# A planned attention and gated feed-forward kernel: new rules for the order of down's sums and of the weight pieces, two more v tiles, and an output weight that is split in the middle of the run

## The chip, the cores and the metric

The kernel runs on one core of one Trainium2 chip. The metric is the time of one execution in microseconds on the device, as the median of several runs. The core's engines are TensorE (PE in the profile, with its weight loads as PEld), VectorE (DVE), ScalarE (ACT), GpSimd (POOL) and SyncE (SP, which here issues nearly all transfers, in one order).

## What is computed

The input x has 2048 rows of 576 numbers, in fp32.

```python
xn = layernorm(x)
q, k, v = split(xn @ wqkv)                    # 32 heads of 18 columns
s = concat(softmax(q @ k.T * 18**-0.5) @ v) @ wo
g = silu(((xn @ w_gate) * (xn @ w_up)) @ w_down)   # inner width 4608
out = x + s * g
```

## The kernel before, in words

Every fp32 operand of a product is held as a high and a low part (`hi` is a rounded copy, made by ScalarE; `lo` is the rest, made by a subtraction on GpSimd or VectorE), and a product is the sum of hi·hi, lo·hi and hi·lo.

**Prologue.** x is normalised and turned into columns, q, k and v are computed with the whole array (`qk_block`, `v_block`). The 16 blocks of v come in the order 0 to 3, 8 to 15, 4 to 7; block t goes through one of three SBUF tiles, `vbox[t % 3]` (L389), is copied there by ScalarE (L391) and stored to `sv` by SP (L393). Between those stores SP also issues the loads of x's columns in their two-half layout (`x_first`, L417).

**Main phase.** `order()` (L1046) is a planner that runs while the program is built. It keeps a modelled clock for each of the two row halves of TensorE's array (`clk[0]`, `clk[1]`), a modelled time at which each other engine is free (`free`) and at which each PSUM bank is free (`banks`), and writes out the matmuls one after another. The work that it places:

- *gate and up*, in 72 units (4 chunks of 512 rows by 18 groups of 256 inner columns) of two column blocks n each. Up runs on half 0 (`up_end`, ScalarE drains the bank), gate on half 1 (`gate_end`, VectorE multiplies, then ScalarE and GpSimd split the product into `hs`). One block is 27 matmuls of 512 columns per half (L618).
- *down*, 8 sums per unit, each of 6 matmuls of 288 columns on half 0 and then 6 on half 1 into the same bank (L664). An instruction on a third engine (L668) hands the bank from one half to the other. `down_end` drains the bank: VectorE adds to `acc` (L721), or ScalarE copies (L715) and GpSimd adds (L684).
- *a items*: scores for the row maxima, mostly on half 0 (L530; VectorE reduces, L532). *b items*: the scores again, mostly on half 1 (L569; ScalarE takes the exponential, L571). Each kind has two PSUM banks of its own. a and b are paced by goals (`a_goal`, `b_goal`) so that they last over the whole phase.
- *visits*: up to six blocks of probabilities times v, on the whole array (L580).

Gate, up, down and visits share four PSUM banks (`banks["g"]`). `pick` (L1032) chooses between the streams of one half: it prefers gate or up while `54 * (g's unit - d's unit - 1) + 27 * (block) + step < FROM + STEP * sum`, with `FROM, STEP = 54, 0`; otherwise down. `can_go` (L982) says what may start; a new sum of down waits while three of the four banks are held or more than one sum is being handed over (`WAITING`).

**Weights.** In the first 18 units the weights come raw from HBM. A list, `chores`, holds their splitting in pieces: three per gate/up block (L205, L206), two per down unit (L236, L237), each followed by a step that stores the split tile for the later chunks and loads the next raw one (L211, L241). `small` (L912) takes one from the list when the modelled ScalarE is free within 0.1 us:

```python
eng, length = KINDS.get(q[0][0].__name__, ("POOL", 0.0))
if eng == "POOL" or free[eng] <= now + 0.1 + (0.15 * (now - quiet[0]) if q is later else 0.0):
```

When a matmul is written that needs weights whose pieces have not been placed, `ready` (L159) places them all at that point, without telling the modelled clocks (`gu_start`, L611; `down_start`, L657). A second list, `later`, holds less urgent steps (`silu`).

**End.** After the last gate block, `wo_prepare` (L761) loads the output weight raw and splits it on ScalarE (L771) and VectorE (L772). Then 16 blocks of rows are projected (L1187), multiplied and added (L1197, L1198), and stored.

Of the kernel before, what the change touches and what calls it, by code (L numbers as in the profile page):

```python
# [40 lines left out]
def kernel(  # L41
# [34 lines left out]
    sv = dram.tile([S, H, DH + 1], FT, name="sv")  # L76
    so = dram.tile([S, D], FT, name="so")
    sg = dram.tile([S, D], FT, name="sg")

    turns = [0]  # L80

# [63 lines left out]


    chores, later = [], []

    def chore(all=True):
        q = (all and chores) or later  # L150
# [30 lines left out]
    def g_get(n):  # L181

        if n == 2 * len(units):
            u = n // 2 - 1
            dw[u] = wpool.tile([128, 2, 2, D], FR, name="wdl", tag="wgu", bufs=2)
            nc.sync.dma_start(dw[u].bitcast(FT), swd[columns_of(u)])
            ddone.add(u)
        if n >= 2 * len(units):
            return
        f = 2 * columns_of(n // 2) + n % 2  # L190
        if n > 1 and n // 2 % NF2 == 0:
            gw[n] = gw[n - 2]
            gdone.add(n)
            return
        w = gw[n] = g_tile()
        if n >= 2 * NF2:
            nc.sync.dma_start(w.bitcast(FT), swg[f])
            gdone.add(n)
            return
        if n not in graw:  # L200
            ready(gdone, n - 2)
        raw = graw.pop(n)

        def piece(b):
            nc.scalar.activation(w[:, b:b + 3, :], raw[:, b:b + 3, :], AF.Copy)  # L205
            nc.gpsimd.tensor_tensor(w[:, 9 + b:12 + b, :], raw[:, b:b + 3, :], w[:, b:b + 3, :].bitcast(FT),  # L206
                                    op=OP.subtract)

        def end():
            gdone.add(n)  # L210
            nc.sync.dma_start(swg[f], w.bitcast(FT))  # L211
            g_load(n + 2)

        chores.extend([(piece, (b,)) for b in (0, 3, 6)] + [(end, ())])
# [5 lines left out]
    def d_get(n):  # L220
        if n >= len(units) - 1:
            return
        p = columns_of(n)
        if n and n % NF2 == 0:
            dw[n] = dw[n - 1]
            ddone.add(n)
            return
        w = dw[n] = d_tile()
        if n >= NF2:
            nc.sync.dma_start(w.bitcast(FT), swd[p])  # L230
            ddone.add(n)
            return
        raw = draw.pop(n)

        def piece(k):
            nc.scalar.activation(w[:, k, 0, :], raw[:, k], AF.Copy)  # L236
            nc.gpsimd.tensor_tensor(w[:, k, 1, :], raw[:, k], w[:, k, 0, :].bitcast(FT), op=OP.subtract)  # L237

        def end():
            ddone.add(n)  # L240
            nc.sync.dma_start(swd[p], w.bitcast(FT))  # L241
            d_load(n + 1)

        chores.extend([(piece, (k,)) for k in range(2)] + [(end, ())])

    R = 3 * DH
    PT = 13
# [109 lines left out]
    vbox = {}  # L357

    def v_fetch(h):
        raw = vp.tile([128, 5, HALF], FT, name="wvraw", bufs=1)  # L360
# [7 lines left out]
    def v_split(h):  # L368
        if h == 0:
            vbox["w"] = vp.tile([128, 10, D], FR, name="wv")  # L370
            for i in range(3):
                vbox[i] = vp.tile([128, H, DH + 1], FT, name=f"vo{i}")
                nc.gpsimd.memset(vbox[i], 1.0)
        raw, wv = vbox["raw"], vbox["w"]
        cs = slice(h * HALF, (h + 1) * HALF)
        for k, d, lo in ((0, 0, 4), (1, 1, 5), (2, 2, 6), (3, 3, 7), (4, 8, 9)):
            nc.scalar.activation(wv[:, d, cs], raw[:, k, :], AF.Copy)
            nc.gpsimd.tensor_tensor(wv[:, lo, cs], raw[:, k, :], wv[:, d, cs].bitcast(FT),
                                    op=OP.subtract)

    def v_block(t):
        c, r = divmod(t, 4)
        ps = [bank("g", 3), bank("g", 3)]
        for h in range(2):
            for n, (a, e) in enumerate(PAIRS):
                nc.tensor.matmul(ps[h][:, 0:HALF], xcs[c][:, e, r * 128:(r + 1) * 128],  # L386
                                 vbox["w"][:, a, h * HALF:(h + 1) * HALF], start=n == 0,
                                 stop=n == len(PAIRS) - 1)
        v = vbox[t % 3]  # L389
        for h in range(2):  # L390
            nc.scalar.activation(v[:, 16 * h:16 * h + 16, 0:DH],  # L391
                                 ps[h][:, 0:HALF].rearrange("p (a b) -> p a b", b=DH), AF.Copy)
        nc.sync.dma_start(sv[t * 128:(t + 1) * 128], v)  # L393
# [68 lines left out]
    for i in range(2):  # L462
        qs.append(stk.tile([128, S], FR, name=f"qs{i}"))
        ks.append(stk.tile([128, S], FR, name=f"ks{i}"))
        nc.gpsimd.memset(ks[i].bitcast(FT), 1.0)
    g_load(0)
    g_load(1)
    d_load(0)
# [29 lines left out]
    for t in range(4, 8):  # L498
        v_block(t)
        chore()  # L500
    assert n == 18
    pro.close()
    vstack.close()

# [7 lines left out]
    with ExitStack() as mid:  # L512
# [106 lines left out]
                             stop=k == len(TERMS) - 1)  # L619

        def up_end(n, ps):
            us[n] = mp.tile([128, 512], FT, name="us", bufs=1)
            nc.scalar.activation(us[n], ps, AF.Copy)  # L623

# [99 lines left out]
        def down_summed(u, s):  # L724
            c, q = units[u]
            if q == NF2 - 1 and c < NCH - 1:
                seen[c, s] = seen.get((c, s), 0) + 1
                if seen[c, s] == 2:
                    silu_store(4 * c + s)

        def silu(t, new, end):

# [25 lines left out]

        wos = {}

        def wo_prepare():  # L761
            raw = xcp.tile([128, 8, D], FT, name="wor", tag="xc")
            nc.sync.dma_start(raw[:, 0:4, :], wo[0:512, :].rearrange("(k p) c -> p k c", p=128))
            for b in (0, 64):
                nc.sync.dma_start(raw[b:b + 64, 4, :], wo[512:576, :])
            wos[0] = xcp.tile([128, 8, D], FR, name="wos", tag="xc")
            wos[1] = wpool.tile([128, 2, D], FR, name="wos2", tag="wgu", bufs=2)

            def piece(k):
                hi, lo = (wos[0][:, k, :], wos[0][:, 4 + k, :]) if k < 4 else (wos[1][:, 0, :], wos[1][:, 1, :])  # L770
                nc.scalar.activation(hi, raw[:, k, :], AF.Copy)  # L771
                nc.vector.tensor_tensor(lo, raw[:, k, :], hi.bitcast(FT), op=OP.subtract)  # L772

            chores.extend([(piece, (k,)) for k in range(5)])

        passed = {}

        def stream(r, kind):

            def glu(n):  # L780
                c, q = units[n // 2]
                box = []
                for k in range(len(TERMS)):
                    def work(k=k):
# [6 lines left out]
                        if k == len(TERMS) - 1:  # L791
                            (gate_end if r else up_end)(n, box[0])
                            if r and n == 2 * len(units) - 1:
                                wo_prepare()
# [31 lines left out]
        TOTAL = H * N  # L826
        LEAD, MOST, AHEAD, MANY = 24, 40, PT - 1, 6
        PACE, SKEW, PULL, FIRST = 1.005, 1.0, 3.0, 0.4
        FROM, STEP, WAITING = 54, 0, 1
        slots, gone = {}, [0.0, 0.0]  # L830
        clk, free = [0.0, 0.0], {"DVE": 0.0, "ACT": 0.0, "POOL": 0.0}
        banks = {"a": [0.0] * 2, "b": [0.0] * 2, "g": [0.0] * 4}
        turn = {"a": 0, "b": 0}

# [30 lines left out]
        def a_next(r=0):  # L865
# [7 lines left out]
            a_item(h, i, r)  # L873
            slot = turn["a"] % 2
            turn["a"] += 1
            banks["a"][slot] = engine("DVE", clk[r] + 0.45, 0.70) + 0.06
            clk[r] += 0.229
            na += 1
            if i == N - 1:
# [8 lines left out]
        def b_next(r=1):  # L888
# [10 lines left out]
            slot = turn["b"] % 2  # L899
            turn["b"] += 1  # L900
            end = engine("ACT", clk[r] + 0.45, 0.60)
            banks["b"][slot] = end + 0.06
            clk[r] += 0.229
            nb += 1
            if i % 4 == 3:
                due.append((h, i // 4, end + 0.1))

        KINDS = {"piece": ("ACT", 0.55), "first": ("ACT", 0.70), "second": ("DVE", 0.45), "inverse": ("DVE", 1.06)}

        quiet = [0.0]  # L910

        def small(now):  # L912

            q = chores or later
            if q is later and now < quiet[0]:
                return
            if q:
                eng, length = KINDS.get(q[0][0].__name__, ("POOL", 0.0))
                if eng == "POOL" or free[eng] <= now + 0.1 + (0.15 * (now - quiet[0]) if q is later else 0.0):
                    if eng != "POOL":  # L920
                        done = engine(eng, now, length)
                        if q[0][0].__name__ == "piece":
                            engine("POOL", done + 0.1, 1.05)
                    elif q[0][0].__name__ == "last":
                        engine("POOL", now, 1.5)
                    if not chores:
                        quiet[0] = now + (16.0 if q[0][0].__name__ == "last" else 6.0)
                    chore()

        def rows(job):  # L930
# [48 lines left out]

        upped, gated, downed = {}, {}, {}  # L980

        def can_go(r, first, ev):  # L982

            kind, n, k = ev
            now = clk[r]
            if kind == "d":
                if r and not alone(n, k // 6):
                    return k % 6 or handed.get((n, k // 6), 1e9) <= now
                if first and (sum(t >= 1e9 for t in banks["g"]) >= 3 or len(handed) > WAITING):
                    return False  # L990
                return k or (there.get(("h", n), 1e9) <= now and (n < 1 or downed.get(n - 1, 1e9) <= now))
            u = n // 2
            c, q = units[u]
            if k == 0:
                if n > 1 and loaded.get(n - 2, 1e9) > now:
                    return False
                if r and ahead[0] - ahead[1] < FIRST and heads[0]["g"] is not None:
                    return False
# [231 lines left out]
```

## Time and profile before

| | us |
|---|---|
| median of 3 runs | 2736.94 (2736.72 to 2739.9) |
| the profiled execution | 2743.11 |
| its span, first to last instruction | 2741.1 |
| busy: PE, PEld | 2666.4, 2181.3 |
| busy: DVE, ACT, POOL | 1825.9, 1571.0, 651.9 |

How to read it: a busy PE is not a PE at its peak. With two halves of the array at work, an instruction of one half alone counts as busy as one of each. The row PEclk tells the clock that TensorE was granted in each slice of the span. In the views quoted below, "A <- B: t, n, m" says that A waited for B t microseconds in total, n times, m at the longest; a row of the view by stage has, for each engine, busy microseconds with the number of instructions in brackets, then granted clock, share of the DMA engines, and GB/s.

### The profile page before, as it was taken

What the parts mean: (1) busy time and instruction counts of PE and PEld (TensorE: products, weight loads), DVE (VectorE), ACT (ScalarE), POOL (GpSimd) and SP (SyncE); (2) the same over time, 40 slices, a digit from 0 to 9 for tenths busy, and PEclk for the clock granted to TensorE, in tenths of its full rate; (3) what the DMA queues carried; (4) which work ended last, traced back from release to release, by engine and by line L of the source; (5) the groups of instructions that cost most, each with busy time, mean ns of one, the idle gap of its engine ahead of it and who ended that gap; (6) DMA issues with size and microseconds to landing.
All of it is one profiled execution on the core that took longest, in us unless ns stands there. A gap on an engine that the chain in (4) does not pass through costs nothing.

```text
span 2741.1 us, 59194 instructions
## 1 busy us (share of the span) xinstructions
PE 2666.4 (97%) x24504; PEld 2181.3 (80%) x24504; DVE 1825.9 (67%) x3012; ACT 1571.0 (57%) x3096; POOL 651.9 (24%) x671
## 2 busy tenths in 40 slices
PE   7998999989899999999999999999999999999999
PEld 6897887767677887788778778888887888887779
DVE  7207776656566777776677777777777777777336
ACT  4222666656565666566655666666666666666652
POOL 3113534433331111111111112111111122211115
PEclk9999999989899999999999999999999999999999
DMA  7797757756565453544454445444456444443346
GB/s 218 228 288 213 209 152 198 191 147 147 163 155 152 133 149 124 144 131 124 146 137 133 124 151 147 140 140 137 146 138 151 138 144 136 144 144 108 122 141 215
DMA packets 199805, 428.40 MB, mean 156 GB/s; under 512 B 80976, under 2 KB 130544, under 8 KB 166128
## 3 DMA queue, kind: packets, MB, share of 16 engines
q1 hardware_dynamic: 197296, 416.36, 51.4%
q0 software_dynamic: 2240, 8.26, 0.8%
q8 instruction: 192, 3.15, 0.5%
q14 instruction: 77, 0.63, 0.1%
HBM read 311.69 MB, written 107.61 MB: 153 GB/s over the span
## 4 chain that ended last, share of the span: by engine, by line
PE 92%; DMA 3%; DVE 2%; SPq 1%; ACT 1%; POOL 1%; issue 1%; POOLq 0%; ACTq 0%; DVEq 0%
PE pg L618 33%; PE pg L580 17%; PE pg L664 15%; PE pa L530 11%; PE pb L569 9%; PE pg L1187 2%; PE pg L386 2%; PE pa L332 1%; PE pb L332 1%; SPq L417 1%; DMA wgu<-swg 1%; POOL wd L237 1%; DMA ks<-sqk 1%; ACT pt L571 0%; DVE xn L294 0%
## 5 line engine op out<-in xcount | busy, mean ns | idle before, releaser
L532 DVE TENSOR_REDUCE mx<-pa 128x1 f32<-128x512 f32 x2048 | 1374.9, 687 | 350.9 <-PE pa L530 199.9
L618 PE MATMUL pg<-xc,wgu 64*128 64x512 f32 x7776 | 1478.3, 396 | 24.7 <-ACT vo L391 12.3
L571 ACT ACTIVATE pt<-pb 128x512 f32<-128x512 f32 x2048 | 1168.0, 597 | 560.3 <-PE pb L569 399.9
L618 PEld LDWEIGHTS pg<-xc,wgu 64*128 64x128 f32 x7776 | 1093.9, 188 | 70.5 <-ACT vo L391 12.6
L664 PE MATMUL pg<-wd,hs 64*128 64x288 f32 x6816 | 886.5, 297 | 19.9 <-ACT wd L236 10.1
L664 PEld LDWEIGHTS pg<-wd,hs 64*128 64x128 f32 x6816 | 814.9, 188 | 42.5 <-POOL wd L237 14.3
L569 PE MATMUL pb<-qs,ks 56*128 56x512 f32 x2048 | 814.5, 407 | 0.3 <-ACT pt L571 0.2
L530 PE MATMUL pa<-ks,qs 54*128 54x512 f32 x2048 | 809.4, 403 | 0.0
L580 PE MATMUL pg<-pt,vt 128*32 128x512 f32 x4096 | 463.9, 599 | 6.0 <-DVE us L630 2.7
L530 PEld LDWEIGHTS pa<-ks,qs 54*128 54x128 f32 x2048 | 374.8, 186 | 77.7 <-issue 66.2
L640 POOL TENSOR_TENSOR hs<-us,hs 128x512 fp32r<-128x512 f32 x144 | 185.8, 1290 | 991.2 <-ACT hs L633 806.7
L569 PEld LDWEIGHTS pb<-qs,ks 56*128 56x128 f32 x2048 | 372.5, 185 | 25.9 <-ACT pt L571 10.8
L684 POOL TENSOR_TENSOR acc<-acc,st 128x288 f32<-128x288 f32 x268 | 216.2, 808 | 617.2 <-ACT st L715 324.5
L580 PEld LDWEIGHTS pg<-pt,vt 128*32 128x32 f32 x4096 | 123.9, 110 | 288.7 <-issue 272.9
L586 DVE TENSOR_TENSOR oc<-oc,pg 128x512 f32<-128x512 f32 x64 | 44.0, 687 | 306.7 <-PE pg L580 306.7
L633 ACT ACTIVATE hs<-us 128x512 fp32r<-128x512 f32 x144 | 91.0, 632 | 118.9 <-DVE us L630 118.7
L721 DVE TENSOR_TENSOR acc<-acc,pg 128x288 f32<-128x288 f32 x277 | 123.5, 447 | 48.1 <-PE pg L664 43.9
L206 POOL TENSOR_TENSOR wgu<-wraw,wgu 128x384 fp32r<-128x384 f32 x108 | 107.5, 1012 | 195.0 <-ACT wgu L205 145.2
L630 DVE TENSOR_TENSOR us<-pg,us 128x512 f32<-128x512 f32 x144 | 98.7, 685 | 50.0 <-PE pg L618 40.4
L715 ACT ACTIVATE st<-pg 128x288 f32<-128x288 f32 x268 | 109.9, 410 | 37.3 <-PE pg L664 22.8
L623 ACT ACTIVATE us<-pg 128x512 f32<-128x512 f32 x144 | 85.8, 595 | 39.5 <-PE pg L618 34.0
L584 ACT ACTIVATE oc<-pg 128x512 f32<-128x512 f32 x32 | 19.1, 598 | 132.8 <-PE pg L580 132.8
(105 smaller groups left out, 1148.9 us busy)
## 6 DMA issues: line engine op xcount, KB each, us to landing
wgu<-swg SPq DMA_DIRECT2D x102, 1152.0 KB
wd<-swd SPq DMA_DIRECT2D x50, 1152.0 KB
swg<-wgu SPq DMA_DIRECT2D x36, 1152.0 KB
qs<-sqk SPq DMA_DIRECT2D x192, 144.0 KB
ks<-sqk SPq DMA_DIRECT2D x192, 144.0 KB
swd<-wd SPq DMA_DIRECT2D x18, 1152.0 KB
sqk<-hl SPq DMA_DIRECT2D x32, 512.0 KB
xc<-sx SPq DMA_DIRECT2D x48, 256.0 KB
```

The source lines that it names most:

```text
L206: nc.gpsimd.tensor_tensor(w[:, 9 + b:12 + b, :], raw[:, b:b + 3, :], w[:, b:b + 3, :].bitcast(FT), op=OP.subtract)
L530: nc.tensor.matmul(p, q[rows, t * 128:(t + 1) * 128], k[rows, c * 512:(c + 1) * 512], start=True, stop=True)
L532: nc.vector.tensor_reduce(mx[h][:, t, c:c + 1], p, axis=AX.X, op=OP.max)
L569: nc.tensor.matmul(p, k[rows, t * 128:(t + 1) * 128], q[rows, c * 512:(c + 1) * 512], start=True, stop=True)
L571: nc.scalar.activation(pt[t, c // 2][:, c % 2, :], p, AF.Exp, scale=scale)
L580: nc.tensor.matmul(p[32 * c:32 * c + 32, :], vt[h // 2][:, t, 6 * (h % 2):6 * (h % 2) + 32], pt[t, c // 2][:, c % 2, :], start=t == ts[0], ...
L618: nc.tensor.matmul(ps, gw[n][half[r], a, :], xg[i][half[r], e, :], start=k == 0, stop=k == len(TERMS) - 1)
L640: nc.gpsimd.tensor_tensor(hj[:, 1, :], h32, hj[:, 0, :].bitcast(FT), op=OP.subtract)
L664: op = nc.tensor.matmul(ps[:, 0:HALF], hs[u][half[r], j, a, s * 128:(s + 1) * 128], dw[u][half[r], j, e, i * HALF:(i + 1) * HALF], start=( ...
L684: nc.gpsimd.tensor_tensor(a, a, st, op=OP.add)
L715: nc.scalar.activation(st, ps[:, 0:HALF], AF.Copy)
L721: nc.vector.tensor_tensor(a, a, ps[:, 0:HALF], op=OP.add)
```

## The change

1. *Two more v tiles.* The tiles stand in a list `vrows`; two more are made (in a pool that closes when the prologue ends) after the first four blocks, and the tile of a block follows a counter in place of `t % 3`.
2. *Pieces urgent.* While `chores` is not empty, the allowance grows with the time since it was last empty or served (`quiet[1]`). A down piece has its own entry (0.71 us on ScalarE, 1.47 on GpSimd). The time at which the split will be over is kept in `split_at`, and `can_go` starts neither a block of gate or up nor a unit of down before it.
3. *Down spread.* `FROM, STEP = 8, 4.5`: sum s of a unit is preferred to gate and up from step 8 + 4.5·s of the next unit. A sum starts only if `room()`: two banks free now, or one, with at least `LEFT = 4` steps to go in both running blocks. `WAITING` is gone.
4. *Banks of a and b* count as free 0.18 us after the draining engine's end in place of 0.06.
5. *Output weight early.* After the silu of row block 3, five steps of `later` each fetch 128 rows of wo, split them (ScalarE, then GpSimd in two pieces) and store both parts to a new DRAM tensor `swo`. After the last gate block only `swo` is loaded.
6. `up_end` first places GpSimd's waiting low parts (`lows`).

```diff
     def v_block(t):
-        v = vbox[t % 3]
+        v = vrows[vturn[0] % len(vrows)]
+        vturn[0] += 1
...
+    more_rows(vmore.enter_context(tc.tile_pool(name="vmore", bufs=1, side="right")), 2)
...
         def end():
             gdone.add(n)
+            split_at["g", n] = free["POOL"] + 0.2
             nc.sync.dma_start(swg[f], w.bitcast(FT))
             g_load(n + 2)
...
         def up_end(n, ps):
+            while lows:
+                pool_now()
             us[n] = mp.tile([128, 512], FT, name="us", bufs=1)
...
+        def wo_split(k):
...
+            def fetch():
+                w = wpool.tile([128, 2, D], FR, name="wor", tag="draw", bufs=1)
...
+            def whole():
+                nc.scalar.activation(box[0][:, 1, :], box[0][:, 0, :].bitcast(FT), AF.Copy)
+
+            def rest(i):
+                w = box[0][:, :, i * HALF:(i + 1) * HALF]
+                nc.gpsimd.tensor_tensor(w[:, 0, :], w[:, 0, :].bitcast(FT), w[:, 1, :].bitcast(FT), op=OP.subtract)
+
+            def keep():
+                for i, j in ((1, k if k < 4 else 8), (0, 4 + k if k < 4 else 9)):
+                    nc.sync.dma_start(swo[:, j, :], box[0][:, i, :].bitcast(FT))
+
+            later.extend([(fetch, ()), (whole, ()), (rest, (0,)), (rest, (1,)), (keep, ())])
+
+        def wo_fetch():
             wos[0] = xcp.tile([128, 8, D], FR, name="wos", tag="xc")
+            nc.sync.dma_start(wos[0].bitcast(FT), swo[:, 0:8, :])
             wos[1] = wpool.tile([128, 2, D], FR, name="wos2", tag="wgu", bufs=2)
+            nc.sync.dma_start(wos[1].bitcast(FT), swo[:, 8:10, :])
...
-        FROM, STEP, WAITING = 54, 0, 1
+        FROM, STEP, LEFT = 8, 4.5, 4
...
-            banks["a"][slot] = engine("DVE", clk[r] + 0.45, 0.70) + 0.06
+            banks["a"][slot] = engine("DVE", clk[r] + 0.45, 0.70) + 0.18
...
-            banks["b"][slot] = end + 0.06
+            banks["b"][slot] = end + 0.18
...
-                if eng == "POOL" or free[eng] <= now + 0.1 + (0.15 * (now - quiet[0]) if q is later else 0.0):
+                if eng == "POOL" or free[eng] <= now + 0.1 + 0.15 * (now - quiet[0] if q is later else now - quiet[1]):
...
+        def room():
+
+            at = clk[0]
+            loose = sum(t <= at for t in banks["g"])
+            if loose > 1:
+                return True
+            left = [len(TERMS) - h["g"][4][2] if h["g"] and h["g"][4][2] else 0 if h["g"] else 99 for h in heads]
+            return loose == 1 and min(left) >= LEFT
...
-                if first and (sum(t >= 1e9 for t in banks["g"]) >= 3 or len(handed) > WAITING):
+                if first and not room():
+                    return False
+                if k == 0 and (n not in ddone or split_at.get(("d", n), 0.0) > now):
                     return False
...
             if k == 0:
-                if n > 1 and loaded.get(n - 2, 1e9) > now:
+                if n not in gdone or split_at.get(("g", n), 0.0) > now or n > 1 and loaded.get(n - 2, 1e9) > now:
                     return False
```

More of the change, by code (lines that the diff above doesn't have):

```diff
@@ L78 @@
     sg = dram.tile([S, D], FT, name="sg")
+    swo = dram.tile([128, 10, D], FT, name="swo")
     turns = [0]
@@ L147 @@
     chores, later = [], []
+    clk, free, split_at = [0.0, 0.0], {"DVE": 0.0, "ACT": 0.0, "POOL": 0.0}, {}
     def chore(all=True):
@@ L233, in d_get, with big_piece @@
         raw = draw.pop(n)
-        def piece(k):
+        def big_piece(k):
             nc.scalar.activation(w[:, k, 0, :], raw[:, k], AF.Copy)
@@ L240, in end @@
             ddone.add(n)
+            split_at["d", n] = free["POOL"] + 0.2
             nc.sync.dma_start(swd[p], w.bitcast(FT))
             d_load(n + 1)
-        chores.extend([(piece, (k,)) for k in range(2)] + [(end, ())])
+        chores.extend([(big_piece, (k,)) for k in range(2)] + [(end, ())])
     R = 3 * DH
@@ L355, in x_block, with more_rows @@
                 nc.sync.dma_start(xg[i][r:r + 64, k:k + 2, :].bitcast(FT), sx[c, b])
-    vbox = {}
+    vbox, vrows, vturn = {}, [], [0]
+    def more_rows(pool, n):
+        for _ in range(n):
+            vrows.append(pool.tile([128, H, DH + 1], FT, name=f"vo{len(vrows)}"))
+            nc.gpsimd.memset(vrows[-1], 1.0)
     def v_fetch(h):
@@ L370, in v_split @@
             vbox["w"] = vp.tile([128, 10, D], FR, name="wv")
-            for i in range(3):
-                vbox[i] = vp.tile([128, H, DH + 1], FT, name=f"vo{i}")
-                nc.gpsimd.memset(vbox[i], 1.0)
+            more_rows(vp, 3)
         raw, wv = vbox["raw"], vbox["w"]
@@ L465 @@
         nc.gpsimd.memset(ks[i].bitcast(FT), 1.0)
+    vmore = ExitStack()
+    more_rows(vmore.enter_context(tc.tile_pool(name="vmore", bufs=1, side="right")), 2)
     g_load(0)
@@ L501 @@
     assert n == 18
+    vmore.close()
     pro.close()
@@ L729, in down_summed @@
                     silu_store(4 * c + s)
+                    if 4 * c + s == 3:
+                        for k in range(5):
+                            wo_split(k)
         def silu(t, new, end):
@@ L759 @@
         wos = {}
[L761 to L765, printed above, removed]
+        def wo_split(k):
+            box = []
+            def fetch():
+                w = wpool.tile([128, 2, D], FR, name="wor", tag="draw", bufs=1)
+                box.append(w)
+                if k < 4:
+                    nc.sync.dma_start(w[:, 0, :].bitcast(FT), wo[128 * k:128 * k + 128, :])
+                else:
+                    for b in (0, 64):
+                        nc.sync.dma_start(w[b:b + 64, 0, :].bitcast(FT), wo[512:576, :])
+            def whole():
[8 more added lines that the diff above has]
+        def wo_fetch():
             wos[0] = xcp.tile([128, 8, D], FR, name="wos", tag="xc")
+            nc.sync.dma_start(wos[0].bitcast(FT), swo[:, 0:8, :])
             wos[1] = wpool.tile([128, 2, D], FR, name="wos2", tag="wgu", bufs=2)
[L769 to L774, printed above, removed]
+            nc.sync.dma_start(wos[1].bitcast(FT), swo[:, 8:10, :])
         passed = {}
@@ L793, in work @@
                             if r and n == 2 * len(units) - 1:
-                                wo_prepare()
+                                wo_fetch()
                     end = (("DVE", 0.70) if r else ("ACT", 0.60)) if k == len(TERMS) - 1 else None
@@ L828 @@
         PACE, SKEW, PULL, FIRST = 1.005, 1.0, 3.0, 0.4
-        FROM, STEP, WAITING = 54, 0, 1
+        FROM, STEP, LEFT = 8, 4.5, 4
         slots, gone = {}, [0.0, 0.0]
-        clk, free = [0.0, 0.0], {"DVE": 0.0, "ACT": 0.0, "POOL": 0.0}
         banks = {"a": [0.0] * 2, "b": [0.0] * 2, "g": [0.0] * 4}
@@ L906, in b_next @@
                 due.append((h, i // 4, end + 0.1))
-        KINDS = {"piece": ("ACT", 0.55), "first": ("ACT", 0.70), "second": ("DVE", 0.45), "inverse": ("DVE", 1.06)}
-        quiet = [0.0]
+        KINDS = {"piece": ("ACT", 0.55), "big_piece": ("ACT", 0.71), "first": ("ACT", 0.70), "second": ("DVE", 0.45), "inverse": ("DVE", 1.06), "whole": ("ACT", 0.71)}
+        quiet = [0.0, 0.0]
         def small(now):
+            if not chores:
+                quiet[1] = now
             q = chores or later
@@ L917, in small @@
             if q:
-                eng, length = KINDS.get(q[0][0].__name__, ("POOL", 0.0))
-                if eng == "POOL" or free[eng] <= now + 0.1 + (0.15 * (now - quiet[0]) if q is later else 0.0):
+                name = q[0][0].__name__
+                eng, length = KINDS.get(name, ("POOL", 0.0))
+                if eng == "POOL" or free[eng] <= now + 0.1 + 0.15 * (now - quiet[0] if q is later else now - quiet[1]):
                     if eng != "POOL":
                         done = engine(eng, now, length)
[L922 to L927, printed above, removed]
+                        if name in ("piece", "big_piece"):
+                            engine("POOL", done + 0.1, 1.05 if name == "piece" else 1.47)
+                    elif name in ("last", "rest"):
+                        engine("POOL", now, 1.5 if name == "last" else 0.85)
+                    if chores:
+                        quiet[1] = now
+                    else:
+                        quiet[0] = now + (16.0 if name == "last" else 6.0)
                     chore()
```

## The prediction

> **What bounds the kernel now.** First the page: the span, the engines, the clock by slices.
>
> ```profile
> span 2741.1 us, 59194 instructions
> PE 2666.4 (97%) x24504; PEld 2181.3 (80%) x24504; DVE 1825.9 (67%) x3012; ACT 1571.0 (57%) x3096; POOL 651.9 (24%) x671
> PEclk9999999989899999999999999999999999999999
> ```
>
> TensorE is the bound, and its digits of clock dip in the first third only. So I read the view by stages next.
>
> ```profile
> 217.00:222.00 5.00, 5.00 (x24) 5.00 (x26) 2.15 (x4) 0.01 (x1) 0.00 (x0) 0.52 0.96 289
> 230.00:580.00 350.00, 341.13 (x3243) 285.56 (x3240) 249.92 (x406) 209.73 (x421) 153.11 (x148) 0.98 0.68 188
> 580.00:915.00 335.00, 310.90 (x2757) 241.93 (x2759) 209.00 (x339) 200.25 (x395) 101.51 (x99) 0.93 0.55 148
> 915.00:1400.00 485.00, 481.48 (x4600) 387.33 (x4595) 355.10 (x579) 295.36 (x568) 87.33 (x91) 1.00 0.45 139
> 1400.00:1900.00 500.00, 499.20 (x4828) 403.20 (x4823) 369.18 (x602) 308.06 (x596) 90.44 (x92) 1.00 0.46 139
> 1900.00:2400.00 500.00, 499.30 (x4885) 405.27 (x4879) 370.94 (x602) 310.42 (x603) 93.27 (x96) 1.00 0.48 144
> ```
>
> Before 915 us, while raw weights are being split, PE stands idle 350 - 341.1 + 335 - 310.9 = 33.0 us, and the clock that is missing is worth 0.02 x 350 + 0.07 x 335 = 30.5 us more. Behind that PE hardly stops: 1485 us hold 5.0 us of idle time. What it waits for, over the whole run (first row) and between 230 and 915 us (the others):
>
> ```profile
> PE pg L618 <- ACT vo L391: 12.3, 1, 12.3
> ...
> PE pg L664 <- ACT wd L236: 10.1, 8, 2.3
> PE pg L664 <- POOL wd L237: 9.9, 11, 1.1
> PE pg L618 <- ACT wgu L205: 6.7, 5, 2.5
> ...
> PE pg L618 <- POOL wgu L206: 2.1, 5, 0.6
> ```
>
> Splitting costs 10.1 + 9.9 + 6.7 + 2.1 = 28.8 us of idle PE. One such event, by the timeline of ScalarE and GpSimd and by windows:
>
> ```profile
> 726.19 4.86 ACT L571 ACTIVATE pt<-pb 128x512 f32<-128x512 f32 x8 [0.24 <-PE pb L569]
> ...
> 731.89 1.28 ACT L236 ACTIVATE wd<-draw 128x576 fp32r<-128x576 f32 x2
> 732.73 2.77 POOL L237 TENSOR_TENSOR wd<-draw,wd 128x576 fp32r<-128x576 f32 x2 [10.53 <-ACT wd L236]
> ...
> 731.00:734.00 3.00, 0.61 (x3) 0.19 (x2) 0.72 (x2) 2.16 (x5) 1.27 (x1) 0.96 0.00 0
> 734.00:738.00 4.00, 3.81 (x22) 3.43 (x23) 1.38 (x2) 0.93 (x2) 1.50 (x2) 0.50 0.46 184
> ```
>
> Eight exponentials run back to back while the raw weights lie ready and GpSimd has been idle for 10.53 us; both pieces come together, only when PE already needs them. That is the forced placing by `ready`: the list starved because ScalarE was never free within 0.1 us. And after PE's pause the clock is 0.50.
>
> **The change part by part.** The planner's clocks are not executed, only its order is. A rule that is too cautious therefore costs only where it puts a worse order, not the time that it models.
>
> *Two more v tiles.* The chain and the timeline around the one long wait:
>
> ```profile
> 207.54 8.46 DMA sv<-vo
> ...
> 207.54 9.62 SPq L393 DMA_DIRECT2D sv<-vo  x4
> 216.11 0.71 ACT L391 ACTIVATE vo<-pg 128x288 f32<-128x288 f32 x2 [14.41 <-DMA sv<-vo]
> 216.87 0.79 PE L618 MATMUL pg<-xc,wgu 64*128 64x512 f32 x1 [12.32 <-ACT vo L391]
> ```
>
> The last block (t = 7, the 16th) reuses the tile of the 13th, whose store SP issues at 207.54, behind the loads of x's columns. With five tiles it reuses that of the 11th, stored before those loads. The 12.3 us go, and with them the half clock after them, 5.0 x (1 - 0.52) = 2.4. Late next could be those loads, issued by SP until just before the store; at the store's 8.46 us they land near 212, and only the last 3 of a block's 27 steps read the last of them. I take 13 of 14.7; bounds 5 (the loads end the wait instead) and 14.7.
>
> *Pieces urgent, starts that wait for the split.* Nothing is added to PE. The pieces (0.52 and 0.68 us on ScalarE, 1.01 and 1.41 on GpSimd, from the rows below) are as many as before, only earlier.
>
> ```profile
> L205 ACT ACTIVATE wgu<-wraw 128x384 fp32r<-128x384 f32 x81 | 39.5, 522 | 0.0
> L236 ACT ACTIVATE wd<-draw 128x576 fp32r<-128x576 f32 x30 | 19.7, 684 | 0.0
> L206 POOL TENSOR_TENSOR wgu<-wraw,wgu 128x384 fp32r<-128x384 f32 x36 | 35.7, 1009 | 59.3 <-ACT wgu L205 50.7 <-PE pg L618 3.2 <-issue 1.9
> L237 POOL TENSOR_TENSOR wd<-draw,wd 128x576 fp32r<-128x576 f32 x14 | 19.6, 1414 | 40.2 <-ACT wd L236 33.2 <-DMA swg<-wgu 4.5 <-issue 2.4
> ```
>
> Behind an early piece on ScalarE queue exponentials, and the b items wait for these; an upper bound is the pieces' whole time between 300 and 915 us, 39.5 + 19.7 = 59 us, but ScalarE is busy only 60% of 580 to 915 (200.25 of 335) and b items have two banks, so I take 0. Is there work in place of the stalled matmuls? a and b, which may run ahead of their goals. If the 335 us shrink to 295, VectorE's 209 are 71%, below the 74% (369.18 of 500) that later stages carry without idle PE. I take 85% of 28.8, 24 us; the rest for pieces that GpSimd ends late. Of the 30.5 us of clock I leave out a fifth, which falls on time that was idle anyway, and take 85% of the rest, 20 us. Bounds: 0 and 59.3.
>
> The Trainium skill, "TensorE: Matmul & The Clock Gate", section "HAM oscillation — how this bites in real kernels", gives as its rule that PE's idle gaps should not exceed about 3.4 us. The trace does not bear that out as a threshold: waits of 2.5 us and less are followed by a clock of 0.50. By the rule alone these waits would cost no clock, and the forecast would be 20 us higher.
>
> *Down spread, `room`, banks of a and b at 0.18 us.* An example of what steals time without idle PE:
>
> ```profile
> 2280.97 1.26 ACT L571 ACTIVATE pt<-pb 128x512 f32<-128x512 f32 x2 [0.33 <-PE pb L569]
> 2281.21 0.19 PEld L618 LDWEIGHTS pg<-xc,wgu 64*128 64x128 f32 x2
> 2281.62 0.18 PEld L569 LDWEIGHTS pb<-qs,ks 56*128 56x128 f32 x1 [0.22 <-ACT pt L571]
> ```
>
> The b item stands in PE's queue before the exponential has left its bank, and everything behind it waits. To size this I take undisturbed runs from the chain, and the counts from 915 to 2400 us:
>
> ```profile
> 1908.93 1.37 PE pg L618 x12
> 2445.09 5.29 PE pg L580 x48
> 2645.91 1.58 PE pg L664 x22
> ...
> L618 PE MATMUL pg<-xc,wgu 64*128 64x512 f32 x4706 | 904.0, 393 | 1.4 <-DMA wgu<-swg 1.4
> L664 PE MATMUL pg<-wd,hs 64*128 64x288 f32 x4224 | 553.0, 294 | 0.0
> L569 PE MATMUL pb<-qs,ks 56*128 56x512 f32 x1323 | 524.5, 404 | 0.0
> L530 PE MATMUL pa<-ks,qs 54*128 54x512 f32 x1318 | 517.3, 401 | 0.0
> L580 PE MATMUL pg<-pt,vt 128*32 128x512 f32 x2686 | 301.4, 594 | 3.6 <-DVE us L630 1.2 <-DVE acc L721 0.8 <-DVE acc L719 0.4
> ```
>
> 1.37 / 12 is 114 ns for a 512-column matmul of a half, 1.58 / 22 is 72 for one of down, 5.29 / 48 is 110 in a visit. So (4706 + 1323 + 1318) x 0.114 + 4224 x 0.072 + 2686 x 0.110 = 1437 of 1485 us; 48 are lost, 79 over the 2443 us of the main phase. Three visits per head make 96, and if each costs one matmul at its edges (0.594 us), 57 of the 79 stay. I take 20 for stalls that the later banks and drains spread over the unit remove; bounds 79 and, the other way, the slower rival below. Down's weights must now be reloaded between the start of one unit's last sum and that of the next unit's first, 54 - 7 x 4.5 = 22 steps; `can_go` still tests for it, and gate and up go on meanwhile. The low parts placed before `up_end` cost nothing: same instructions.
>
> *Output weight.* The chain at the end, and the transfers between 2640 and 2680 us in 40 slices:
>
> ```profile
> 2659.13 1.72 DVE wos L772 x3
> ...
> GB/s 406 424 392 357 392 408 293 51 21 12 0 0 0 0 0 0 0 0 1 128 145 59 166 143 277 371 376 387 279 290 288 270 281 366 394 376 348 408 411 403
> ```
>
> VectorE's split stands in front of down's last additions: 2 us gained. The new load is 128 x 10 x 576 x 4 = 2.95 MB, 7.6 us at 390 GB/s, and DMA is nearly idle there. In mid-run it adds five copies (0.68 us) and ten subtractions on GpSimd (24% busy) and 16 issues on SP: 0.
>
> Sum: 13 + 24 + 20 + 20 + 2 = 79. The profiled execution took 2743.1, 6 above the median of 2736.94; from the median: **2658**.
>
> **The rivals.**
>
> *The order gains nothing:* weights and v as above, no gain after 915 us: 2737 - 59 = 2678. For it: PE is 99.9% busy there. The clock rule named above would give the same time, with half clocks due to something else.
>
> *The pieces stay late:* served one by one with ScalarE full, the list is still forced at the unit's start: 2737 - 13 - 2 - 10 = 2712, with half of the gain of the order. Against it: the allowance grows 0.15 us per us, and 5 us make up a whole exponential.
>
> *Slower: down's halves lose their partners.* A sum goes through half 0, a third engine, half 1; both halves now follow their own step counts and a bank rule. Where the other half has nothing at that moment, a down matmul costs 144 ns in place of 72. Of 6912, a quarter alone costs 124 us: 2737 - 59 + 124 = 2802. It decides from 59 / 498 = 12% on. Against it: a, b, gate and up are there as fillers in every unit.
>
> **How the numbers follow.** Forecast 0.50, order without gain 0.20, late pieces 0.10, no change 0.05, slower 0.15. About 0.2% (5 us) is what a measurement of this kernel can tell from no change. Faster 0.80, same 0.05, slower 0.15. The range goes from 2608 (v 15, weights 59, end 2, two thirds of the 79) to 2715, just above the late pieces; it leaves out the last two cases.
>
> **What would show it.** Right: no wait of L618 on L391 near 205 us; the waits of L664 and L618 on L236, L237, L205 and L206 below 5 us in sum; a clock of 1.00 in every stage after 230; down's matmuls in more, shorter runs; PE reaching the projection some 75 us sooner. Wrong: GpSimd or DMA in those waits' place, or over 1485 us for the same counts of matmuls with PE still 99% busy.

## The result and the profile after

The changed kernel takes 2673.31 us (median of 4 runs, 2671.45 to 2678.21) against 2738.14: a ratio of 0.9766 with a 95% interval of 0.9749 to 0.9783, 64.8 us less. The profiled execution took 2672.76 us, with a span of 2671.0. Lines after the edits have moved: gate and up are L629, down L677, a L541 and b L580, their drains L543 and L582, visits L591, down's addition on VectorE L734 (on ScalarE L728), the copy to a v tile L399.

The page of the changed kernel, the rows that were read before:

```profile
PE 2617.8 (98%) x24504; PEld 2165.9 (81%) x24504; DVE 1813.7 (68%) x3007; ACT 1572.0 (59%) x3096; POOL 664.6 (25%) x683
PEclk9999999999999999999999999999999999999999
```

PE has 48.6 us less of busy time for the same 24504 matmuls, and no slice of its clock is below 9 tenths. The stages of the changed kernel:

```profile
217.00:222.00 5.00, 5.00 (x43) 3.92 (x41) 4.84 (x8) 1.23 (x2) 2.40 (x3) 1.00 0.89 165
230.00:580.00 350.00, 348.56 (x3366) 292.27 (x3366) 256.46 (x416) 229.17 (x458) 161.85 (x154) 1.00 0.71 196
580.00:915.00 335.00, 325.60 (x3148) 264.25 (x3142) 238.89 (x391) 218.43 (x432) 99.72 (x96) 0.99 0.60 165
915.00:1400.00 485.00, 478.77 (x4675) 390.87 (x4673) 354.91 (x579) 300.71 (x582) 96.00 (x101) 1.00 0.49 149
1400.00:1900.00 500.00, 495.70 (x4855) 405.38 (x4853) 370.08 (x607) 311.96 (x604) 91.22 (x93) 1.00 0.45 138
1900.00:2400.00 500.00, 495.40 (x4846) 403.48 (x4846) 369.04 (x603) 308.25 (x594) 93.31 (x95) 1.00 0.47 143
```

Between 230 and 915 us PE idles 10.8 us in place of 33.0, and issues 3366 + 3148 = 6514 matmuls in place of 6000. From 915 to 2400 us it idles more than before, 15.1 us in place of 5.0, and yet issues 14376 in place of 14313 (sums of the rows above; a matmul that crosses the edge of a stage is counted in both). What PE waits for longest in the changed kernel after the prologue:

```profile
...
PE pg L591 <- DVE acc L734: 8.3, 13, 1.1
PE pg L629 <- DMA xc<-sx: 5.5, 2, 4.4
PE pg L591 <- ACT st L728: 3.9, 7, 0.6
PE pg L677 <- DMA wd<-swd: 3.4, 3, 1.9
PE pb L1212 <- DMA oin<-so: 3.2, 1, 3.2
...
```

Not one wait for a weight piece or a v tile is left. New, or longer than before, are visits that wait until down's sums have left a bank (12.2 us), a chunk change that waits for x's columns (5.5, before 2.2), down for its weights (3.4) and the first projection for o (3.2).

The chain, where the wait for the v tile was:

```profile
194.89 9.95 PE pg L393 x75
204.87 0.42 ACT vo L399
205.33 1.41 PE pg L629 x7
```

The main phase starts at 205.3 in place of 216.9 us, straight behind the last block of v. At its other end, the timelines of PE before (first fence) and after:

```profile
2661.80 4.78 PE L664 MATMUL pg<-wdl,hs 64*128 64x288 f32 x58 [0.75 <-DVE acc L721]
...
2667.85 2.38 PE L1187 MATMUL pg<-wos,oT 128*128 128x288 f32 x16
```

```profile
2585.73 5.86 PE L677 MATMUL pg<-wdl,hs 64*128 64x288 f32 x77
2594.80 0.66 PE L1212 MATMUL pb<-ident,oin 128*128 128x128 f32 x4 [3.21 <-DMA oin<-so]
...
2596.36 5.36 PE L1235 MATMUL pg<-wos,oT 128*128 128x288 f32 x28
```

Down's last matmul ends at 2591.6 us in place of 2666.6, 75.0 us sooner. What follows takes 79.4 us in place of 74.5: the wait for o, and a first block of the projection that takes 5.4 us in place of 4.0, at a clock of 0.57 between 2596 and 2600 us.

### The profile page after: what moved, and what is told of

Same layout as the page of the kernel before. It is cut to its first block, busy times and chain, and to the rows that moved or that the text cites. A ratio compares the mean times of both kernels' runs of the same rounds, so it can differ in the third digit from the quotient of the medians.

```text
span 2671.0 us, 59265 instructions
## 1 busy us (share of the span) xinstructions
PE 2617.8 (98%) x24504; PEld 2165.9 (81%) x24504; DVE 1813.7 (68%) x3007; ACT 1572.0 (59%) x3096; POOL 664.6 (25%) x683
## 4 chain that ended last, share of the span: by engine, by line
PE 93%; DMA 3%; DVE 2%; ACT 1%; POOL 0%; issue 0%; SPq 0%; POOLq 0%; ACTq 0%; DVEq 0%
PE pg L629 34%; PE pg L591 17%; PE pg L677 15%; PE pa L541 10%; PE pb L580 9%; PE pg L1235 2%; PE pg L393 2%; PE pa L336 2%; PE pb L336 2%; DMA wd<-swd 1%; DMA xc<-sx 1%; DVE mx L543 0%; DVE xn L298 0%; ACT pt L582 0%; DMA ks<-sqk 0%
## 5 line engine op out<-in xcount | busy, mean ns | idle before, releaser
L629 PE MATMUL pg<-xc,wgu 64*128 64x512 f32 x7776 | 1588.6, 392 | 7.3 <-DMA xc<-sx 5.5
L543 DVE TENSOR_REDUCE mx<-pa 128x1 f32<-128x512 f32 x2048 | 1372.0, 687 | 323.0 <-PE pa L541 200.8
L582 ACT ACTIVATE pt<-pb 128x512 f32<-128x512 f32 x2048 | 1175.7, 598 | 481.1 <-PE pb L580 371.1
L629 PEld LDWEIGHTS pg<-xc,wgu 64*128 64x128 f32 x7776 | 1143.8, 186 | 43.0 <-DMA xc<-sx 6.3
L677 PE MATMUL pg<-wd,hs 64*128 64x288 f32 x6816 | 1017.3, 293 | 3.9 <-DMA wd<-swd 3.4
L677 PEld LDWEIGHTS pg<-wd,hs 64*128 64x128 f32 x6816 | 930.3, 186 | 22.4 <-DMA wd<-swd 3.7
L580 PE MATMUL pb<-qs,ks 56*128 56x512 f32 x2048 | 803.3, 400 | 2.3 <-ACT pt L582 1.2
L541 PE MATMUL pa<-ks,qs 54*128 54x512 f32 x2048 | 804.1, 400 | 0.0
L591 PE MATMUL pg<-pt,vt 128*32 128x512 f32 x4096 | 459.3, 594 | 13.8 <-DVE acc L734 8.3
L541 PEld LDWEIGHTS pa<-ks,qs 54*128 54x128 f32 x2048 | 372.2, 184 | 74.7 <-issue 63.0
L580 PEld LDWEIGHTS pb<-qs,ks 56*128 56x128 f32 x2048 | 371.9, 185 | 12.0 <-ACT pt L582 4.7
L591 PEld LDWEIGHTS pg<-pt,vt 128*32 128x32 f32 x4096 | 123.3, 110 | 292.3 <-issue 262.9
L734 DVE TENSOR_TENSOR acc<-acc,pg 128x288 f32<-128x288 f32 x277 | 123.6, 447 | 52.6 <-PE pg L677 50.2
L728 ACT ACTIVATE st<-pg 128x288 f32<-128x288 f32 x268 | 109.9, 410 | 16.0 <-PE pg L677 12.3
```

Of the source, the lines that this page charges most:

```text
L541: nc.tensor.matmul(p, q[rows, t * 128:(t + 1) * 128], k[rows, c * 512:(c + 1) * 512], start=True, stop=True)
L543: nc.vector.tensor_reduce(mx[h][:, t, c:c + 1], p, axis=AX.X, op=OP.max)
L580: nc.tensor.matmul(p, k[rows, t * 128:(t + 1) * 128], q[rows, c * 512:(c + 1) * 512], start=True, stop=True)
L582: nc.scalar.activation(pt[t, c // 2][:, c % 2, :], p, AF.Exp, scale=scale)
L591: nc.tensor.matmul(p[32 * c:32 * c + 32, :], vt[h // 2][:, t, 6 * (h % 2):6 * (h % 2) + 32], pt[t, c // 2][:, c % 2, :], start=t == ts[0], ...
L629: nc.tensor.matmul(ps, gw[n][half[r], a, :], xg[i][half[r], e, :], start=k == 0, stop=k == len(TERMS) - 1)
```

## The experiments

Theory: the v tiles, the pieces and the later banks of a and b each remove waits of their own, and what the order gained after 915 us, it gained by the spread and the banks together. Rival: the spread gives nothing, or costs, and the gain is the banks'. Each kernel was compared with the kernel before, which stood between 2736.9 and 2738.1 us.

| run | kernel | us, median |
|---|---|---|
| e1_three_v | changed, three v tiles | 2686.3 |
| e2_weights_alone | before, with the rules for pieces | 2711.2 |
| e9_old_down_006 | changed, down's order and a/b banks as before | 2692.8 |
| e4_down_as_before | changed, down's order as before | 2665.7 |
| e3_bank006 | changed, a/b banks as before | 2683.4 |
| e7_room_alone | changed, no spread, with `room` | 2703.2 |
| e8_spread_alone | changed, spread, old start rule | 2695.4 |
| e5_wo_late | changed, output weight split at the end | 2670.3 |
| e6_g018 | changed, shared banks at 0.18 too | 2675.6 |
| e10_old_down_g018 | e4, shared banks at 0.18 too | 2650.8 |
| e11_after_pace1004 | changed, PACE 1.004 | 2680.4 |
| e12_old_down_pace1004 | e4, PACE 1.004 | 2648.2 |

**Three v tiles** (e1).

```diff
-    more_rows(vmore.enter_context(tc.tile_pool(name="vmore", bufs=1, side="right")), 2)
```

> The changed kernel with three v tiles in place of five. If the wait of 12.3 us and the half clock behind it were all that the tiles removed, 2673 + 12 to 15 = 2685 to 2688 us, with L629 waiting some 12 us for L398 near 205 us. If the loads of x's columns would have ended that wait anyway, or the later stages take the delay back, below 2680.

2686.29 us, 13.0 more. In its waits the old one is back, beside those that the changed kernel has too:

```profile
PE pg L628 <- ACT vo L399: 13.1, 1, 13.1
```

The two tiles are worth their wait, and no later stage gives it back: the first of the two cases.

**The rules for the pieces alone** (e2): `small`, `split_at` and both tests in `can_go` put into the kernel before, with `up_end` placing the low parts first.

> The kernel before with the rules for the pieces alone (urgency, no start ahead of the split, low parts first). If the order of down plays no part in the first third, the traces' difference there comes back: 2738 - 53 = 2685 us, a clock of 1.00 between 230 and 915 us, under 5 us of waits for pieces. If the pieces come in time only because down is spread (it frees its weights' tile earlier in the unit), half of that or less: 2710 or more, with waits for the down pieces left.

2711.20 us, 25.7 less than before (2736.89 in that measurement): the second of the two cases, by its time. By its trace it is nearly the first. All that PE waited for between 230 and 915 us, and the same stage's row:

```profile
PE pg L621 <- DMA xc<-sx: 3.3, 2, 2.5
PE pb L572 <- DMA qs<-mr: 2.6, 1, 2.6
PE pa L533 <- ACT mr L557: 1.4, 1, 1.4
PE pb L572 <- ACT pt L574: 1.2, 2, 0.7
PE pg L583 <- ACT st L720: 0.8, 1, 0.8
PE pg L583 <- DVE acc L726: 0.3, 1, 0.3
...
230.00:915.00 685.00, 675.16 (x6383) 547.52 (x6382) 492.19 (x801) 434.15 (x871) 260.70 (x249) 0.99 0.66 179
...
915.00:2400.00 1485.00, 1477.63 (x14221) 1189.41 (x14220) 1094.97 (x1782) 914.08 (x1771) 268.14 (x275) 1.00 0.45 138
```

No piece is waited for, with down in its old order, so the spread is not what brings the pieces in time. The stage from 230 to 915 us holds 6383 matmuls where the kernel before had 5997 (same view), about 386 x 0.107 = 41 us of work. But 915 to 2400 holds 14221 against 14297, 8 us less, though of the rules that were put in only that for the low parts reaches into this stage. The sum of both, 33 us, is what separates the two profiled executions (2743.11 and 2708.98); the medians differ by less, because the profiled execution of before lies 6 us above its median and that of e2 2 us below. That the same work came out in another order called for a control.

**Controls** (e11, e12): PACE 1.004 for 1.005 in the changed kernel and in e4.

```diff
-        PACE, SKEW, PULL, FIRST = 1.005, 1.0, 3.0, 0.4
+        PACE, SKEW, PULL, FIRST = 1.004, 1.0, 3.0, 0.4
```

> A control: the changed kernel with PACE 1.004 in place of 1.005, which moves the goals of a and b by a thousandth and has no purpose. If the plan reacts to small moves by its rules alone, 2671 to 2676. If any move shuffles the order, 2660 to 2690, and differences of that size between the other kernels say little of a rule.

> The same control on the version of e4 (down's order as before): 2664 to 2668 if the plan is steady. If the spread is truly worse, it stays below the control of the changed kernel; if the 8 us between them were chance, the two controls may stand either way.

2680.39 and 2648.20 us: 7.1 more and 17.5 less for a change without a purpose. Neither kernel stayed in the range for a steady plan. The plan is sensitive: a single pair of kernels that differ in a planner's rule tells little below some 17 us, however exact the runs. What follows is held to this: by several pairs, or by waits that the trace names.

**The banks of a and b** (e3 with the spread, e9 with down's old order).

```diff
-            banks["a"][slot] = engine("DVE", clk[r] + 0.45, 0.70) + 0.18
+            banks["a"][slot] = engine("DVE", clk[r] + 0.45, 0.70) + 0.06
-            banks["b"][slot] = end + 0.18
+            banks["b"][slot] = end + 0.06
```

> The changed kernel with banks of a and b free 0.06 us after the drain in the plan, as before. If the later banks are what removed stalls of a and b, PE is slower by what these stalls cost before: 2673 + 15 to 25 = 2688 to 2698. If the spread of down removed them, 2673 to 2678.

> The changed kernel with down's order and the banks of a and b (0.06 us) both as before; what is left is v, pieces and output weight. If the later banks are worth 10 us whatever down's order, as with the spread, 2666 + 10 = 2676. If they are only needed with the spread, 2666 to 2669. By the sum of parts alone (v 13, pieces 26 of 2737) it would be 2698.

2683.43 us, 10.1 more than the changed kernel, between the two cases; 2692.83, 27.2 more than e4, which has e9's order of down, and near the sum of the other parts (2698). The mechanism shows in the trace. Counted between 1000 and 2400 us, weight loads of b items that were released by an exponential and begin within 70 ns of its end are 313 of 1245 before and 297 of 1250 in e9, but 87 of 1251 after and 102 of 1266 in e4. Beyond a spacing of 115 ns, they stretch the time from the load ahead of them by 24.7 and 24.0 us against 2.4 and 2.5; in e3 it is 18.4. The part of this that leaves PE's loader idle stands in the waits between 915 and 2400 us, of before, e9 and after:

```profile
PEld pb L569 <- ACT pt L571: 5.6, 31, 0.2
```

```profile
PEld pb L580 <- ACT pt L582: 6.3, 35, 0.2
```

```profile
PEld pb L580 <- ACT pt L582: 1.4, 1, 1.4
```

With 0.06 us there are some thirty such waits in down's old order (and 14, of 4.1 us, in e3, which has the spread); with 0.18 there is one in the changed kernel and none in e4. Not all of the stretch comes back as time. At the prediction's own prices (114 ns for a matmul of 512 columns on one half, 72 for one of down, 110 in a visit) PE does 1446 us of work between 915 and 2400 us in the changed kernel against 1432 in e3, and 1441 in e4 against 1435 in e9. The banks of a and of b were always changed together; what each is worth was not tried.

**Down's order** (e4, and its two halves e7 and e8).

```diff
-        FROM, STEP, LEFT = 8, 4.5, 4
+        FROM, STEP, WAITING = 54, 0, 1
...
-                if first and not room():
+                if first and (sum(t >= 1e9 for t in banks["g"]) >= 3 or len(handed) > WAITING):
```

> The changed kernel with down's order as before (a unit's sums after the next unit, start rule by held banks). If the spread is what gained after 915 us, 2673 + 7 to 20 = 2680 to 2693. If it gives nothing or costs (visits now wait for down's drains, 12.5 us in the changed kernel's trace), 2660 to 2675, and those waits go back below 3 us.

> The changed kernel with FROM and STEP as before (54, 0) and room() kept. If the spread in time is what costs (visits find a bank still being drained, loads for the next chunk queue behind down's), it comes near the kernel with both as before: 2664 to 2668. If room() is what costs, it stays at 2671 to 2676.

> The changed kernel with FROM and STEP of the change (8, 4.5) and the start rule by held banks as before. If the spread in time costs and room() softens it, 2674 to 2690, with more waits of visits for drains than the changed kernel's 13 us. If room() costs, 2662 to 2668.

e4 takes 2665.67 us, 7.6 less than the changed kernel. e7 takes 2703.19 and e8 2695.42, both far worse than either whole: neither expectation, of one half that costs and one that is harmless, holds, and e8's visits wait less for drains (4.9 us) than the changed kernel's 12.2, not more. Four pairs differ in down's order alone. Their medians, and PE's idle time between 915 and 2400 us:

| pair | spread, us | as before, us | idle, spread | idle, as before |
|---|---|---|---|---|
| changed, e4 | 2673.3 | 2665.7 | 15.1 | 2.1 |
| e11, e12: PACE 1.004 | 2680.4 | 2648.2 | 16.0 | 0.3 |
| e6, e10: shared banks at 0.18 | 2675.6 | 2650.8 | 14.9 | 3.5 |
| e3, e9: a/b banks at 0.06 | 2683.4 | 2692.8 | 15.5 | 5.0 |

In the three pairs with the later banks of a and b the spread loses, by 8 to 32 us. In the fourth, with the old banks, it gains 9 us. The idle time is longer with the spread in all four, by 10 to 16 us; e7, with `room` alone, idles 14.2 us there and e8 10.8. The idle time is made of waits that the trace names, while the sign of the whole hangs on the other rules and on chance as large as the controls show. In the same waits, e4 has of the changed kernel's new ones:

```profile
PE pg L591 <- DVE acc L734: 1.8, 4, 0.6
PE pg L591 <- DVE us L643: 1.5, 3, 0.9
PE pg L677 <- ACT st L728: 0.7, 1, 0.7
```

No wait for x's columns, for down's weights or for o. The visits' waits go with the new rule, or with half of it: 12.2 us in the changed kernel, 9.7 in e7, 4.9 in e8, but 1.8 in e4 and 2.2 in e9. Down's wait for its weights goes with the spread: 0.4 to 6.0 us in the seven kernels that have it, and of those with the old order in time only e10 has any (1.1). The wait for x's columns does not. Here are e7 and e9, which have the old order in time, and e3 and e8, which have the spread:

```profile
PE pg L629 <- DMA xc<-sx: 7.8, 3, 7.0
```

```profile
PE pg L629 <- DMA xc<-sx: 5.0, 3, 2.5
```

```profile
PE pg L629 <- DMA xc<-sx: 1.5, 2, 0.7
```

```profile
PE pg L629 <- DMA xc<-sx: 1.6, 2, 1.2
```

In SP's order in the changed kernel, down's weights are stored and loaded anew (748.07 and 749.44 us) among the loads of x's columns; in e4 (724.89 and 725.26) and in e9 (745.79 and 746.21) they go out ahead of them. PE waits in e9 and not in e4, so this place does not explain the wait. Why x's columns come late stays open.

**Output weight** (e5) and **shared banks** (e6, e10).

```diff
-                    if 4 * c + s == 3:
-                        for k in range(5):
-                            wo_split(k)
```

(with `wo_prepare` of before in place of `wo_fetch`), and for e6 and e10:

```diff
-                banks["g"][k] = end + 0.06
+                banks["g"][k] = end + 0.18
```

(and the same for the sums' and the blocks' drains).

> The changed kernel with the output weight loaded raw and split at the end, as before. If the split in front of down's last additions is worth what the chain shows, 2673 + 2 = 2675. If the early split is what delays the end (PE's wait for o's rows of 3.2 us and the half clock behind it are new there), 2668 to 2672, and that wait goes.

> The changed kernel with the four shared banks, too, counted as free 0.18 us after their drain in place of 0.06. If visits wait for down's drains because the plan takes their banks for free too soon, those waits (12.5 us) fall below 5 us and the time to 2660 to 2668. If it only makes the plan more timid (fewer banks free for down), 2673 to 2685.

> The version of e4 (the change with down's order as before) with the shared banks at 0.18 us too. e4 has only 4 us of waits of visits for drains, so by that theory a gain of 0 to 3: 2663 to 2666. If every bank's plan was as much too early as those of a and b (27 us), below 2655.

e5: 2670.25 us, 3.1 less, well inside what the controls move, as was foreseen for an early split that delays the end; the wait for o is gone there. But e4, e6, e7, e8 and e10 to e12 split early too and have no such wait, and e1, e3 and e9 one of 0.9 to 2.1 us. In the changed kernel the last visit ends at 2583.9 us; storing and loading its rows of o lasts until 2594.8, and down's last matmuls cover this only until 2591.6. So the wait hangs on what the plan leaves for the end, and the early split can be called neither a gain nor a loss. e6: 2675.62, the second case, and the visits' largest wait is as before, so it is not the plan's 0.06 that makes visits wait under the spread:

```profile
PE pg L591 <- DVE acc L734: 9.2, 15, 1.1
```

e10: 2650.78, 14.9 less than e4, the second case by its time; the control on the same kernel moved it by 17.5, so this is no proof for the rule.

The fastest version is e12, the change without the spread and without `room`, with the control's PACE of 1.004: 2648.20 us, a ratio of 0.9673 to the kernel before (0.9660 to 0.9686). Of its lead over the changed kernel, 17.5 us came with a change that has no purpose. Its row:

```profile
915.00:2400.00 1485.00, 1484.71 (x14466) 1185.28 (x14466) 1116.74 (x1817) 928.93 (x1813) 276.11 (x287) 1.00 0.47 143
```

0.3 us of idle PE, and 96 matmuls more than the changed kernel's 14370 in the same view.

## Why the prediction was right, step by step

The mechanism was right for the v tiles and the pieces, half right for the order, and did not show for the output weight; the miss of 15 us has three parts. The forecast of 79 us holds almost to the end of the main phase, where the changed kernel is 75.0 us ahead. Then 4.9 us are lost at the projection. And the terms were read from an execution of 2743.1 us but taken off the median of 2736.9: between the two profiled executions 70 us were gained, between the medians 65. Whether those 6 us were part of the waits that went, no trace shows. The pieces gave 49 us of idle time and clock in place of 44, and the order less than its 20; that these nearly cancelled is luck.

- *v tiles, 13 us:* 13.0 by e1. The loads of x's columns were no wait behind it.
- *Pieces, 24 us of idle time and 20 of clock:* right in mechanism. Idle time between 230 and 915 us fell by 22.2, with no wait for a piece left, and the missing clock from 30.5 us to 0.01 x 335 = 3.4. The step is borne out in its own stage, by e2 as well (41 us of work there). As a difference of medians e2 shows 26, for the two reasons given there.
- *The order, 20 us:* this is the term that was mis-sized. The counts of the changed kernel from 915 to 2400 us are

```profile
L629 PE MATMUL pg<-xc,wgu 64*128 64x512 f32 x4771 | 995.4, 392 | 0.0
L677 PE MATMUL pg<-wd,hs 64*128 64x288 f32 x4221 | 640.5, 293 | 3.4 <-DMA wd<-swd 3.4
L580 PE MATMUL pb<-qs,ks 56*128 56x512 f32 x1328 | 520.1, 398 | 1.0 <-DMA qs<-mr 1.0
L541 PE MATMUL pa<-ks,qs 54*128 54x512 f32 x1326 | 519.5, 399 | 0.0
L591 PE MATMUL pg<-pt,vt 128*32 128x512 f32 x2684 | 301.0, 594 | 10.8 <-DVE acc L734 7.0 <-ACT st L728 2.4 <-DVE us L643 0.7
```

  At the prediction's prices this is 1446 us of work in place of 1437, 8.5 us, where 20 us over the main phase of 2443 stood for 12 in this stage. The prediction gave the banks' 0.18 us and the spread one gain between them. The runs part them: the later banks remove the stalls of b that the timeline at 2281 us showed, and gain 10 or 27 us; the spread adds 10 to 16 us of idle time in this stage, and takes 8 to 32 us back with the later banks (with the old ones it gained 9). For the banks' gain the prediction had a line of the trace, for the spread it had none.
- *Down's weights "gate and up go on meanwhile":* not quite, three waits of 3.4 us in sum.
- *Output weight, 2 us:* not seen in the whole. VectorE's pieces are gone from the end, and in e5, where they are back, PE waits 1.9 us for VectorE there; but a wait for o of 3.2 us stands in their place.
- *The rivals:* "the order gains nothing" (2678) came nearer than the forecast (2658), 5 us off against 15. "The pieces stay late" fell. "Slower" did not come, but e7 shows that half of the rule does cost 37 us against e4; whether by halves that lose their partners was not measured.
- *What would show it:* L618's wait and the pieces' waits went as stated, and PE was 75.0 us ahead at down's end and 71 at the projection. The clock was 0.99 in one stage. Taken in order of their starts, down's matmuls between 915 and 2400 us form 2246 unbroken runs in place of 1659, with 1.9 in a run in place of 2.5, as stated. "Wrong: DMA in those waits' place" came true in part, with 5.5 us for x's columns and 3.4 for down's weights; and the same stage with nearly the same counts, the other sign, came half true.
- *The clock rule* (the Trainium skill, "TensorE: Matmul & The Clock Gate", "HAM oscillation — how this bites in real kernels"): with the pieces' waits the half clock behind them went, though none of these waits had reached 3.4 us (the longest was 2.5). The trace stays against reading that figure as a threshold. Where PE paused anew the half clock came too, as behind the wait of 4.4 us that ended at 764.0:

```profile
764.00:770.00 6.00, 5.97 (x36) 5.59 (x38) 2.07 (x3) 2.80 (x5) 0.81 (x1) 0.51 1.03 223
```

## What to carry to other kernels

In a kernel whose order is planned ahead, first remove the waits that the trace names, one by one: the tile returned its 13 us, and the pieces' waits went with the clock behind them. Stalls that hide behind a busy PE returned less: 16 to 22 us of b's stretch went between 1000 and 2400 us, and the work done there rose by 7 to 13 us. A new order is another matter: run a control that changes the plan without a purpose before believing a gain of 1%, and compare every pair that differs in the rule, also the one that goes the other way. Take the terms of a forecast and the time they come off from the same execution. Parts of a change can hide each other: here versions without one part of it are the fastest.

## What the runs showed of the hardware

How long PE may pause before its clock halves could not be read as one number. In the kernel before, a single wait of 1.2 us was followed by a half clock, as its windows show:

```profile
1268.00:1273.00 5.00, 3.77 (x29) 2.85 (x27) 4.18 (x7) 3.48 (x7) 0.00 (x0) 1.00 0.64 139
1273.00:1277.00 4.00, 4.00 (x32) 4.00 (x30) 0.45 (x1) 1.65 (x4) 1.28 (x1) 0.57 0.77 244
```

In the changed kernel a wait of 1.9 us was not:

```profile
1384.00:1388.00 4.00, 2.19 (x17) 1.66 (x14) 2.39 (x4) 1.95 (x4) 1.16 (x1) 1.00 1.05 222
1388.00:1392.00 4.00, 3.95 (x40) 3.34 (x44) 2.82 (x5) 1.70 (x3) 0.00 (x0) 1.00 1.04 231
```

The Trainium skill, "TensorE: Matmul & The Clock Gate", section "What's actually happening", tells of a free-running window of 3.4 us. The trace agrees so far: in the kernel before, after 200 us, the half clock lasts 3.4, 6.8, 10.2 or 13.7 us at a time, and every change of the granted clock falls on one grid of 3.41 us. Whether a pause's place on this grid decides was not tried.
